# A third key tile shared between VectorE and a transfer, moved loads, and a reordered ones product at the seam of attention and MLP

## The chip, the cores and the metric

The kernel runs on one core of one Trainium2 chip. The metric is device time in microseconds (us) for one launch. Before the change the median of three timed runs is 902.75 us (901.11 to 903.17). The profiled execution took 899.86 us, and its trace spans 898.0 us from the first to the last instruction.

## The reference

Bucketed attention is followed by an MLP with a PReLU. With B = 4, H = 8, S = 768 and D = 64:

```python
mask = q_bucket[:, :, :, None] == k_bucket[:, :, None, :]   # 6 sign bits of q @ proj, k @ proj
scores = np.where(mask, scale * np.matmul(q, k.transpose(0, 1, 3, 2)), -1000000000.0)
attn = np.exp(scores - np.max(scores, axis=-1, keepdims=True))
attn = attn / (np.sum(attn, axis=-1, keepdims=True) + 1e-09)
x = np.matmul(attn, v)                                      # to (B*S, H*D) = (3072, 512)
h = x @ w_in                                                # w_in 512 x 2048
g = np.maximum(h, 0.0) + alpha * np.minimum(h, 0.0)
return g @ w_out                                            # w_out 2048 x 512
```

What matters for the change is the row sum of `attn`: for every query, the exponentials over 768 keys have to be added up, and the attention output divided by the result.

## The kernel before

**Attention, 16 pairs.** `fast_path` works through 16 pairs, each one batch entry and two heads (pairs 0 to 3 are batch entry 0). In a pair, TensorE computes scores in 12 cells (6 key tiles of 128 keys by 2 halves of 384 queries). The product of the hash bits and the product of q and k add up in one PSUM tile, and ScalarE writes the exponential (L737) into `pts[kc]`, one tile for each key tile, 128 partitions by 4 rows of 384. Then TensorE multiplies the exponentials with v (`attend`, L768) into the PSUM tile `av`.

**The row sums.** VectorE adds the six key tiles elementwise. `add_first` (L745) puts tiles 0 and 1 into `accp`. For every pair but the first, tile 2 is then added to `accp` by an accumulating transfer that GpSimd issues (L747). `add_last` (L751, L752) puts tiles 3, 4 and 5 into `accd`, and `add_total` (L757) adds `accp` to `accd`. After `attend`, `totals` (L782) sums `accd` over the 128 partitions by a product with ones into the PSUM tile `sm`. `divide` then transposes `sm` (L798), takes reciprocals, and writes the divided output `x` (L815), which is stored to `x_s` in device memory. `divide` of a pair runs on VectorE during the scores of the next pair.

**Buffers around it.** The PSUM tag `sc` has three double banks. Scores, hash bits, turned inputs and `sm` rotate through them, so a later cell of the next pair waits until L798 has read `sm`. `av` has one buffer, so the next `attend` waits for L815.

**Weights.** Between these steps VectorE splits the weights into float32 parts, two pieces of 512 columns per pair (L587 to L624). For `w_in` it also forms sums (L644), which SyncE stores to `w_in_s` (L649).

**The MLP.** Each product is a seven-product scheme over 2 x 2 blocks (`Product.step`; the numbers are those of the seven products). The first product, `ff1(0, 0)`, takes the weight tile `wi` of `load_w(0)` (L846, 896 KB) and four loaded blocks of batch entry 0 (`load_x(0, n)`, L830, 384 KB each: n = 0, 1, 2, 3 give blocks 0, 1, 2, 5). VectorE derives the other three blocks and block 5 anew (`sum_x`, L840): step 0 is block 3 = block 5 - block 0, step 1 is block 5 = block 2 - block 5. Steps 0 and 1 are in pair 13, and steps 2 and 3 in pair 14. Before the change, `load_x` is in pairs 9, 10, 11 and 12 in the order of n, and `load_w(0)`, `load_w(1)` and `load_w(2)` are in pairs 12, 13 and 14.

**What sets the order.** `do(...)` pins an instruction behind the instruction traced before it on its own engine. All VectorE, TensorE and ScalarE work here is pinned, so these engines run in program order. Transfers on SyncE are mostly not pinned and are issued in an order chosen when the kernel is built, but `load_x(0, n)` and the first three `load_w` are pinned behind the transfer written just before them. In pair 13 that is the load of v for pair 15, `load(15, "v")` (L487), which needs the v buffer of pair 13.

**The seam.** In the last pair (15) TensorE does `attend`, then products 1 and 5 of the first MLP block (`now.step(1)`, `now.step(5)`), then `totals(15)`, and after that products 6, 3, 7 and 2. Product 2 (`f_0b`) writes to the PSUM bank that `av` held, so it waits for L815 of pair 15.

Of the kernel before, what the change touches and what calls it, by code (L numbers as in the profile page):

```python
# [12 lines left out]
ALU = mybir.AluOpType  # L13
# [393 lines left out]
def fast_path(  # L407
# [12 lines left out]
    nc = tc.nc  # L420
# [21 lines left out]
    do = tc.keep_in_program_order  # L442
    PE, DVE, ACT, POOL = nc.tensor, nc.vector, nc.scalar, nc.gpsimd
# [36 lines left out]
    accp, accd, av, vsum, sums = {}, {}, {}, {}, {}  # L480
# [102 lines left out]
    def weight_clamp(i):  # L583
        if i < NW:
            i = order[i]
            x = wx[i]
            do(DVE.tensor_scalar(x, x, HI_MIN, None, op0=ALU.max, op1=ALU.max, accum_out=wmax[:, i : i + 1]))  # L587

    def weight_parts(i):
        i = order[i]  # L590
        lo, hi = halves(i)
        x = wx[i]
        wr[i] = r = pool.tile([P, 512], F32, name=f"wr{i}", tag="wr", bufs=1)
        do(DVE.tensor_scalar(
            x.bitcast(U32), x.bitcast(U32), 3, 0xC0000000, op0=ALU.logical_shift_left, op1=ALU.bitwise_xor,
        ))
        do(DVE.tensor_scalar(r.bitcast(U32), x.bitcast(U32), 0x7F800000, None, op0=ALU.bitwise_and))
        do(DVE.scalar_tensor_tensor(r, lo, 2.0 ** -52, r, op0=ALU.mult, op1=ALU.mult))

    def weight_sum(i):  # L600


        i = order[i]
        lo, hi = halves(i)
        x, r = wx[i], wr[i]
        if i < HW:
            n, m = divmod(i, 4)
            if m == 0:
                wst[n] = pool.tile([P, NM, 4, P], F32, name=f"wsi{n}", tag="wsi")
            slot = (0, 5, 1, 2)[m]  # L610
            dst = wst[n][:, slot].rearrange("p i f -> p (i f)")
        else:
            n, m = divmod(i - HW, 2)
            if m == 0:
                wst[HW + n] = pool.tile([P, 4, DM // 2], F32, name=f"wso{n}", tag="wso")
            w = wst[HW + n]
            dst = w[:, 0:4:3] if m == 0 else w[:, 1:3]
        turned = i < HW and m == 3
        do(DVE.scalar_tensor_tensor(
            r, x, -1.0 if turned else 1.0, r, op0=ALU.mult, op1=ALU.subtract if turned else ALU.add,  # L620
        ))
        if i >= HW:
            hi, r = (t.rearrange("p (a f) -> p a f", a=2) for t in (hi, r))
        do(DVE.scalar_tensor_tensor(  # L624
            dst.bitcast(U32), hi, 0x80000000, r.bitcast(U32), op0=ALU.bitwise_and, op1=ALU.bitwise_xor,
        ))
# [99 lines left out]
    def scores(pi, cells):  # L726
        for kc, g in cells:
            sc = two_banks(f"sc{pi}_{kc}_{g}")
            ks = slice(kc * P, (kc + 1) * P)
            qs = slice(g * CW, (g + 1) * CW)  # L730
            for what, first in ((bits, True), (tr, False)):
                for s in range(2):
                    r = slice(D * s, D * s + D)
                    do(PE.matmul(  # L734
                        sc[:, s, :CW], what["k", pi][r, ks], what["q", pi][r, qs], start=first, stop=not first,
                    ))
            do(ACT.activation(pts[kc][:, g, :, :CW], sc[:, :, :CW], AF.Exp, scale=SCALE / DOWN))  # L737


    def p(kc):  # L740
        return pts[kc].rearrange("p g s w -> p (g s) w")[:, :, :CW]

    def add_first(pi):
        accp[pi] = pool.tile([P, 2 * NCH, CW], F32, name=f"accp{pi}", tag="accp", bufs=1)
        do(DVE.tensor_tensor(accp[pi], p(0), p(1), op=ALU.add))  # L745
        if pi:
            nc.gpsimd.dma_start(accp[pi], p(2), accum_op=ALU.add)  # L747

    def add_last(pi):
        accd[pi] = pool.tile([P, 2 * NCH, CW], F32, name=f"accd{pi}", tag="accd", bufs=1)  # L750
        do(DVE.tensor_tensor(accd[pi], p(3), p(4), op=ALU.add))  # L751
        do(DVE.tensor_tensor(accd[pi], accd[pi], p(5), op=ALU.add))  # L752
        if not pi:
            do(DVE.tensor_tensor(accp[pi], accp[pi], p(2), op=ALU.add))

    def add_total(pi):
        do(DVE.tensor_tensor(accd[pi], accd[pi], accp[pi], op=ALU.add))  # L757
# [29 lines left out]
    def divide(pi, between=lambda: None):  # L787

        b, hp = pairs[pi]
        n = HW2 // 32
        a = pool.tile([P, NCH, HW2], F32, name=f"st{pi}", tag="st", bufs=1)
        r = pool.tile([P, NCH, n], F32, name=f"rc{pi}", tag="rc")
        rr = pool.tile([P, NCH, 2, n], F32, name=f"rr{pi}", tag="rr")
        d = pool.tile([P, NCH, CW], F32, name=f"dn{pi}", tag="dn", bufs=1)
        for g in range(NCH):
            do(DVE.transpose(a[:, g], sums[pi][:, g, :HW2]))  # L798
        do(DVE.tensor_scalar(r, a.rearrange("p g (n w) -> p g n w", w=32)[:, :, :, 0], S * EPS, None, op0=ALU.add))
        for h in range(2):  # L800
            do(DVE.reciprocal(rr[:, :, h], r))
        for q0 in (0, D):
            q1 = q0 + 32
            do(POOL.tensor_copy(rr[q0 : q0 + 32, :, 1], rr[q1 : q1 + 32, :, 1]))
            do(POOL.tensor_copy(rr[q1 : q1 + 32, :, 0], rr[q0 : q0 + 32, :, 0]))
        vsum[pi] = pool.tile([P, 1], F32, name=f"vs{pi}", tag="vs")
        do(DVE.tensor_scalar(vsum[pi], av[pi][:, 0, CW : CW + 1], EPS, None, op0=ALU.mult))
        between()
        do(DVE.transpose(
            d.rearrange("p g w -> p (g w)"),  # L810
            rr.rearrange("p g h n -> p (g h n)").unsqueeze(2).to_broadcast([P, 2 * NCH * n, 32]),
        ))

        x = mid.tile([P, NCH, CW], F32, name=f"x{pi}", tag="x", bufs=1)
        do(DVE.scalar_tensor_tensor(x, av[pi][:, :, :CW], vsum[pi], d, op0=ALU.add, op1=ALU.mult))  # L815
        nc.sync.dma_start(x_s[b, hp], x.rearrange("p g w -> p (g w)"))
# [4 lines left out]
    def pinned(when, ins):  # L821

        if when:
            do(ins)

    def load_x(b, *ns):
        for n in ns or range(4):
            m, kh, ch = ((0, 0, 0), (1, 1, 0), (2, 1, 1), (5, 0, 1))[n]
            t = mid.tile([P, 2, CW], F32, name=f"x{b}_{m}", tag=f"x{m}", bufs=1)
            pinned(b == 0, nc.sync.dma_start(  # L830
                t, x_s[b, 2 * kh : 2 * kh + 2].rearrange("k p s -> p k s")[:, :, ch * CW : (ch + 1) * CW],
            ))
            x_m[b, m] = t
# [8 lines left out]
    def load_w(n):  # L842

        if n < B * NI:
            w_m[n] = mid.tile([P, NM, 2, P], F32, name=f"wi{n}", tag="wi", bufs=3)
            pinned(n < 3, nc.sync.dma_start(w_m[n], w_in_s[n % NI]))  # L846
# [285 lines left out]
    for pi in range(NPAIR):  # L1132
        i = 2 * pi

        def weight_begin():
            weight_clamp(i)
            weight_parts(i)
            add_first(pi)

        scores(pi, [c for c in CELLS if pi or c not in ahead])  # L1140
        if pi:
            divide(pi - 1, weight_begin)
        else:
            add_first(pi)
        weight_sum(i)
        weight_group(i)
        load_weight(i + 3)
        if pi == 0:
            weight_abs(1, DVE)
        weight_clamp(i + 1)  # L1150
        add_last(pi)
        weight_parts(i + 1)
        weight_sum(i + 1)
        weight_group(i + 1)
        load_weight(i + 4)
        add_total(pi)
        weight_sums(2)
        if pi + 1 < NPAIR:
            hash_bits(pi + 1)
        if pi + 2 < NPAIR:  # L1160
            turn(pi + 2, "q")
            turn(pi + 2, "k")
        attend(pi)
        if pi + 1 == NPAIR:
            now = ff1(0, 0)
            now.step(1)
            now.step(5)
        totals(pi)
        if pi + 1 == NPAIR:
            divide(pi)  # L1170
        else:
            weight_abs(i + 2)
        if pi + 2 < NPAIR:
            load(pi + 2, "v")
        if 12 <= pi < 15:
            load_w(pi - 12)
        if 9 <= pi < 13:
            load_x(0, pi - 9)
        if pi in (13, 14):
            for n in range(2):  # L1180
                sum_x(0, 2 * pi - 26 + n, DVE)
        if pi == 1:
            setup_alpha()
        for name in "qk":
            magnitude(pi, name)
            if pi + 3 < NPAIR:
                load(pi + 3, name)
        if pi + 1 < NPAIR:
            weight_abs(i + 3)
# [10 lines left out]
    for j, (b, what, n) in enumerate(blocks):  # L1200
# [50 lines left out]
        if j + 1 < len(blocks):  # L1251
            b1, what1, n1 = blocks[j + 1]
            now = ff1(b1, n1) if what1 == "1" else ff2(b1, n1)
# [33 lines left out]
```

## Time and profile before

| what | value | where it is read |
|---|---|---|
| span of the profiled execution, mean granted TensorE clock | 898.0 us, 0.998 | cores |
| one pair, from L745 to L745 (pairs 12 to 13) | 283.57 - 262.96 = 20.61 us | timeline of VectorE |
| end of L757 in pair 13, start of `totals(13)` | 297.38 us, 299.05 us | timelines of VectorE and TensorE |
| end of `attend(14)`, start of `totals(14)` | 318.38 us, 321.97 us | timeline of TensorE |
| start of product 2 of the first MLP block | 348.57 us | timeline of TensorE |
| accumulating transfer of tile 2: issue to landing | 7.5 / 9.1 / 13.6 us (least, median, most of 15) | transfers of L747 |
| its landing in pairs 13, 14 and 15 | 9.0, 13.6 and 7.5 us | the same, by window |

The page has one line per engine with its busy time. The view of waits has one line per pair of a waiting instruction and the one that released it: total time, how often, and the longest. A timeline line has the start, the time from the start of the first to the end of the last instruction, the engine, the line of the kernel, what it writes and reads, and in brackets how long the engine was idle before it and who ended that.

### The profile page before, as it was taken

How to read it: one execution, taken by the hardware profiler on the slowest of the kernel's cores; microseconds unless marked ns; L12 is line 12 of the kernel's file. 1: busy time of each engine (PE TensorE's matmuls, PEld its weight loads, DVE VectorE, ACT ScalarE, POOL GpSimd, SP SyncE). 2: the span in 40 equal slices, each digit the busy share in tenths (PEclk: the TensorE clock that was granted, in tenths of full speed). 3: DMA queues.
4: the chain of work that ended last, by engine and by line, in shares of the span. 5: the costliest groups of instructions: out<-in, count | busy, mean ns of one | idle time of the engine just before them, and what ended most of it. 6: DMA issues, size and time to landing. Idle time of an engine off the chain costs nothing.

```text
span 898.0 us, 15360 instructions
## 1 busy us (share of the span) xinstructions
PE 883.2 (98%) x5886; PEld 594.6 (66%) x5886; DVE 744.0 (83%) x1251; ACT 407.4 (45%) x726; POOL 47.5 (5%) x109
## 2 busy tenths in 40 slices
PE   9999999999999989999999999999999999999996
PEld 5444455555545445557997557997557997556996
DVE  5888878878888986899898668988668988768985
ACT  7888888888888852222112222112222112222111
POOL 0100001101100001120000000000000000000000
PEclk9999999999999999999999999999999999999999
DMA  8576797797898954487333435343525242520241
GB/s 226 133 191 169 186 255 187 175 251 194 206 261 232 293 125 168 167 285 289 132 121 108 162 107 169 108 145 89 179 89 190 96 156 80 166 106 0 95 157 58
DMA packets 128817, 146.06 MB, mean 163 GB/s; under 512 B 77776, under 2 KB 112864, under 8 KB 125152
## 3 DMA queue, kind: packets, MB, share of 16 engines
q1 hardware_dynamic: 116368, 123.90, 43.7%
q0 software_dynamic: 10224, 20.19, 10.5%
q8 instruction: 48, 0.79, 0.4%
q10 hardware_dynamic: 2144, 0.92, 0.4%
q14 instruction: 33, 0.27, 0.1%
HBM read 104.87 MB, written 28.31 MB: 148 GB/s over the span
## 4 chain that ended last, share of the span: by engine, by line
PE 53%; DMA 3%; DVE 3%; issue 1%; SPq 0%; POOL 0%; ACT 0%; DVEq 0%; POOLq 0%; ACTq 0%
PE z_3a L868 2%; PE z_6a L868 2%; PE z_5a L868 2%; PE f_2a L868 2%; PE f_1a L868 2%; PE z_2a L868 2%; PE f_3a L868 2%; PE z_7a L868 2%; PE f_0a L868 2%; PE z_1a L868 2%; PE z_4a L868 2%; PE f_7a L868 2%; PE f_6a L868 2%; PE f_5a L868 2%; PE f_4a L868 2%; DMA w_out_s<-wo 2%
## 5 line engine op out<-in xcount | busy, mean ns | idle before, releaser
L737 ACT ACTIVATE pt<-sc 128x768 f32<-128x768 f32 x192 | 154.9, 812 | 37.6 <-PE sc L734 37.4
L734 PE MATMUL sc<-qT,kT 64*128 64x384 f32 x768 | 155.2, 482 | 0.0
L768 PE MATMUL av<-pt,vn 128*32 128x385 f32 (+1 forms) x1536 | 127.4, 486 | 0.0
L768 PEld LDWEIGHTS av<-pt,vn 128*32 128x32 f32 x1536 | 48.7, 109 | 71.1 <-issue 70.1
L734 PEld LDWEIGHTS sc<-qT,kT 64*128 64x128 f32 x768 | 68.1, 187 | 39.2 <-issue 39.0
L921 DVE TENSOR_TENSOR g<-g,g 128x384 f32<-128x384 f32 x128 | 68.4, 555 | 2.2
L734 PE MATMUL sc<-qb,kb 64*128 64x384 bf16 x384 | 63.3, 323 | 0.3 <-DVE kb L719 0.2
L985 DVE TENSOR_TENSOR gs<-g,gs 128x768 f32<-128x768 f32 x56 | 53.3, 952 | 1.0
L985 DVE TENSOR_TENSOR gs<-g 128x768 f32<-128x768 f32 x56 | 53.3, 951 | 0.0
L977 DVE TENSOR_TENSOR ws<-wl 128x512 f32<-128x512 f32 x56 | 38.5, 688 | 17.4 <-DMA wl<-w_out_s 15.9
L917 DVE SCALAR_TENSOR_TENSOR g<-h,alpha 128x384 f32<-128x384 f32 x32 | 19.7, 617 | 26.1 <-ACT h L910 26.1
L734 PEld LDWEIGHTS <-kb 64*128 64x128 bf16 x384 | 19.0, 94 | 28.1 <-issue 4.3
L745 DVE TENSOR_TENSOR accp<-pt,pt 128x1536 f32<-128x1536 f32 x16 | 28.1, 1758 | 10.1 <-ACT pt L737 10.1
L712 ACT ACTIVATE qb<-hs,hb 32x384 bf16<-32x384 f32 x60 | 34.4, 573 | 1.1
L757 DVE TENSOR_TENSOR accd<-accd,accp 128x1536 f32<-128x1536 f32 x16 | 28.1, 1755 | 8.1 <-DMA accp<-pt 8.1
L752 DVE TENSOR_TENSOR accd<-accd,pt 128x1536 f32<-128x1536 f32 x16 | 28.1, 1758 | 1.7
L751 DVE TENSOR_TENSOR accd<-pt,pt 128x1536 f32<-128x1536 f32 x16 | 28.0, 1753 | 0.0
L723 ACT ACTIVATE kb<-hs,hb 64x384 bf16<-64x384 f32 (+1 forms) x45 | 26.0, 577 | 0.6
L798 DVE STREAM_TRANSPOSE st<-sm 128x192 f32<-128x192 f32 x32 | 10.3, 361 | 18.4 <-PE sm L782 18.4
L868 PE MATMUL f_0a<-x,wi 128*128 128x384 f32 x64 | 23.5, 489 | 0.0
L868 PE MATMUL f_5a<-x,wi 128*128 128x384 f32 x64 | 23.3, 486 | 0.0
L868 PE MATMUL f_2a<-x,wi 128*128 128x384 f32 x64 | 23.3, 486 | 0.0
(351 smaller groups left out, 1775.8 us busy)
## 6 DMA issues: line engine op xcount, KB each, us to landing
wi<-w_in_s SPq DMA_DIRECT2D x32, 896.0 KB, 4.7
wl<-w_out_s SPq DMA_DIRECT2D x16, 1024.0 KB, 4.8
wl<-w_out_r SPq DMA_DIRECT2D x12, 1024.0 KB, 4.8
accp<-pt POOLq DMA_DIRECT2D x15, 768.0 KB, 9.1
raw<-in_moe_w_out_dram SPq DMA_DIRECT2D x16, 512.0 KB, 6.9
raw<-in_moe_w_in_dram SPq DMA_DIRECT2D x16, 512.0 KB, 4.7
w_in_s<-wsi SPq DMA_DIRECT2D x16, 448.0 KB, 5.8
vn<-in_v_dram SPq DMA_DIRECT2D x16, 384.0 KB, 4.5
```

Of the source, the lines that this page charges most:

```text
L712: do(ACT.activation(bits["q", pi][D * s : D * s + 32, cols], ps["q"][c : c + 32, 0 if engine is DVE else half, :CW], AF.Sign, bias=hb[c : ...
L734: do(PE.matmul(sc[:, s, :CW], what["k", pi][r, ks], what["q", pi][r, qs], start=first, stop=not first,))
L737: do(ACT.activation(pts[kc][:, g, :, :CW], sc[:, :, :CW], AF.Exp, scale=SCALE / DOWN))
L745: do(DVE.tensor_tensor(accp[pi], p(0), p(1), op=ALU.add))
L751: do(DVE.tensor_tensor(accd[pi], p(3), p(4), op=ALU.add))
L752: do(DVE.tensor_tensor(accd[pi], accd[pi], p(5), op=ALU.add))
L757: do(DVE.tensor_tensor(accd[pi], accd[pi], accp[pi], op=ALU.add))
L768: do(PE.matmul(av[pi][D * s + t : D * s + t + 32, g, :w], nat["v", pi][:, s, kc * D + t : kc * D + t + 32], pts[kc][:, g, s, :w], start=(k ...
L868: do(PE.matmul(self.ps[bank], self.left(left, k), self.right(right, k), start=start and k == 0, stop=k == self.nk - 1, skip_group_check=no ...
L921: do(DVE.tensor_tensor(new_g(b, to)[:, i], g_m[b, x][:, i], g_m[b, y][:, i], op=ALU.subtract))
L977: do(DVE.tensor_tensor(t, w2[b, n, x], w2[b, n, y], op=op))
L985: do(DVE.tensor_tensor(t, g2[b, n, x], g2[b, n, y], op=ALU.subtract))
```

## The change

It has three parts. In pairs 1 to 15 the transfer adds only rows 2 and 3 of the third key tile, and VectorE adds rows 0 and 1 in a new step `add_third`, ahead of `add_last`. In pair 0 VectorE adds all four rows as before, only earlier. Second, the loads of the first MLP product go to other pairs: `load_w` to pairs 9, 11 and 15, `load_x` to pairs 10 (n = 0), 12 (n = 1 and 3) and 13 (n = 2). Third, in the last pair the ones product comes between products 1 and 5 of the first MLP block instead of after both. It is meant to let the sums of a pair depend on a smaller transfer, to keep large loads out of the pairs in which other transfers are many, and to give the last `divide` more time before product 2.

```diff
         if pi:
-            nc.gpsimd.dma_start(accp[pi], p(2), accum_op=ALU.add)
+            nc.gpsimd.dma_start(accp[pi][:, 2:], p(2)[:, 2:], accum_op=ALU.add)
 ...
-        if not pi:
-            do(DVE.tensor_tensor(accp[pi], accp[pi], p(2), op=ALU.add))
+
+    def add_third(pi):
+        n = 2 if pi else 4
+        do(DVE.tensor_tensor(accp[pi][:, :n], accp[pi][:, :n], p(2)[:, :n], op=ALU.add))
 ...
         weight_clamp(i + 1)
+        add_third(pi)
         add_last(pi)
 ...
             now = ff1(0, 0)
             now.step(1)
-            now.step(5)
         totals(pi)
         if pi + 1 == NPAIR:
+            now.step(5)
             divide(pi)
 ...
-        if 12 <= pi < 15:
-            load_w(pi - 12)
-        if 9 <= pi < 13:
-            load_x(0, pi - 9)
+        if pi in (9, 11, 15):
+            load_w((9, 11, 15).index(pi))
+        if pi in (10, 12, 13):
+            load_x(0, *{10: (0,), 12: (1, 3), 13: (2,)}[pi])
         if pi in (13, 14):
             for n in range(2):
                 sum_x(0, 2 * pi - 26 + n, DVE)
```

## The prediction

> **What bounds the kernel now.** I read the page first, then the waits of TensorE, then the timelines of pairs 13 to 15. The page and the waits of TensorE:
>
> ```profile
> PE 883.2 (98%) x5886; PEld 594.6 (66%) x5886; DVE 744.0 (83%) x1251; ACT 407.4 (45%) x726; POOL 47.5 (5%) x109
> ...
> PE sm L782 <- DVE accd L757: 3.6, 1, 3.6
> ...
> PE f_0b L868 <- DVE x L815: 0.4, 1, 0.4
> ```
>
> TensorE is busy in 98% of the span, so only its idle time can be won. The change can touch two of its waits: 3.6 us once, where the ones product waits for the sums, and 0.4 us once, at product 2. The pairs follow each other at 20.61 us, which is TensorE's own work. VectorE at 83% has gaps in every pair.
>
> The long wait is in pair 14. The timeline of VectorE around it:
>
> ```profile
> 297.30 1.41 DVE L644 TENSOR_TENSOR wsi<-wsi 128x512 f32<-128x512 f32 x2
> 298.62 1.94 DVE L840 TENSOR_TENSOR x<-x,x 128x768 f32<-128x768 f32 x2
> 300.49 0.64 DVE L798 STREAM_TRANSPOSE st<-sm 128x192 f32<-128x192 f32 x2
> ...
> 304.18 1.76 DVE L745 TENSOR_TENSOR accp<-pt,pt 128x1536 f32<-128x1536 f32 x1 [0.23 <-ACT pt L737]
> ...
> 320.06 1.76 DVE L757 TENSOR_TENSOR accd<-accd,accp 128x1536 f32<-128x1536 f32 x1 [3.73 <-DMA accp<-pt]
> ```
>
> L757 was ready at 320.06 - 3.73 = 316.33 and would have ended at 318.08, just before `attend(14)` ended at 318.38. It waited for the transfer of tile 2, which took 13.6 us here against a median of 9.1. SyncE shows what was in its way:
>
> ```profile
> 298.73 3.02 SPq L649 DMA_DIRECT2D w_in_s<-wsi  x3
> 301.85 0.82 SPq L487 DMA_DIRECT2D vn<-in_v_dram  x1
> 302.71 0.49 SPq L846 DMA_DIRECT2D wi<-w_in_s  x1
> 303.25 0.53 SPq L649 DMA_DIRECT2D w_in_s<-wsi  x1
> 303.82 0.76 SPq L846 DMA_DIRECT2D wi<-w_in_s  x1
> ```
>
> Four stores of 448 KB, a load of v and two weight loads of 896 KB go out in 5 us. The last line counts twice over: `load_w(2)` is written in pair 14 but issued here. Last, the weight loads of TensorE:
>
> ```profile
> 301.18 0.10 PEld L734 LDWEIGHTS <-kb 64*128 64x128 bf16 x2 [0.19 <-DVE st L798]
> ```
>
> The third cell of pair 14 waits for L798 of pair 13, because `sm` holds one of three banks. Anything that delays L798 there stops TensorE two cells into the pair.
>
> [...] L747, issued by GpSimd, took 13.6 us in the crowd of pair 14 and 7.5 in pair 15. [...] Here the gap of 3.59 us was followed by cells at the usual 0.81 us[...].
>
> **Part 1, half of the third tile.** VectorE gains 15 adds of 128x768, 15 x 0.95 = 14.3 us in all. In an ordinary pair this is hidden: in pair 13 L757 ends at 297.38 and TensorE takes the sums at 299.05, 1.67 us later, and 0.72 is left after 0.95. The next thing on VectorE, L798, waits for `sm` anyway (18.4 us over 13 pairs). Tile 2 is long written when `add_third` runs. The halved transfer has 384 KB. I have no row for it, and bound its landing by the v loads of that size (about 4 us) and by today's median of 9.1 us. Even the latter ends before L757. It removes the six waits of L757 (8.1 us), of which only that of pair 14 reached TensorE. I assume that `add_third` does not wait for the transfer, since they touch different rows. That halves of one tile can be waited for separately, the trace suggests at the start, where the first halves of q are turned at 4.15 us and the second at 7.06.
>
> **Part 2, the moved loads.** Pair 14 loses two weight loads (1.8 MB) from its front; the loads now in pairs 9 to 12 have 20 us or more until use and cost nothing. One does not: block 2 is now loaded in pair 13, and `sum_x` step 1 of the same pair reads it. That is a new wait on VectorE. Behind it are L798, then L815, which frees `av`, and all sums of pair 14. TensorE's third cell waits for L798. The steps:
>
> - The load is pinned behind that of v for pair 15, whose buffer is free when `attend(13)` ends, at about 299.0. In pairs 9 and 10 the block load followed v by 0.76 and 0.64, so it goes out at 299.7 if no store is ahead.
> - Landing took 4.3, 5.1 and 4.7 us in pairs 9 to 11 (8.3 beside a weight load in pair 12; 3.2 is the least of 16). With 4.6 it lands at 304.3.
> - Without that wait, step 1 would start at 298.71 + 0.95 (`add_third` of pair 13) + 0.94 = 300.6. It waits 3.7 us. After its 0.95, L798 starts at 305.25 instead of 300.49.
> - From L798 to the ready L757 was 316.33 - 300.49 = 15.84. The idle 0.23 ahead of L745 goes, the new add brings 0.95: 16.56. With L757's 1.75 the sums are ready at 323.56. In the kernel before it was 320.06 + 1.76 = 321.82. That is +1.74.
> - TensorE by itself would be there sooner: the third cell to the end of `attend(14)` took 318.38 - 301.44 = 16.9, less than 18.3.
>
> **Part 3, the ones product.** It starts one product earlier (1.39 us), so L815 comes that much sooner and the 0.42 us before product 2 can go. Two things take back part. VectorE has no gap in pair 15 (321.82 to 340.92 = 19.10), and with 0.95 more it needs 20.05, while TensorE reaches the ones product after 18.48 + 1.39 = 19.87: a tie. And ScalarE copies product 5 some 0.78 us later, with 1.8 us of squares (L687) behind it and then the copy of product 6, for which product 7 waits: about 0.2. I take -0.2 in all; the bounds are 0 and -0.42.
>
> **Sum.** Change = landing of block 2 - 302.76 us: (landing + 0.95 + 18.31) - 321.82 - 0.2. At 304.3 it is +1.5, from 902.75 to **904.3 us**.
>
> **The rivals.**
>
> - *A, as above*: v and block 2 go out ahead of the stores. For it: before, VectorE's sums let the stores start at 298.73, just ahead of v; 0.95 us more on VectorE puts the stores behind. 904.3 us. Chance 0.42.
> - *B, stores first*: the order of SyncE is fixed when the kernel is built, and before three stores lead, each about 1.0 us. They would now start at 299.66. With one ahead block 2 lands at 306.1 (+3.3); with three it goes out at 303.6 and lands after 4.6 to 6.9 (what the weight load in that place took), at 308.2 to 310.5: +5.4 to +7.7. I take +5.0, 907.8. [...] Chance 0.30.
> - *C, the wait is hidden*: block 2 is there by 300.6. Then L798 starts at 301.54 and the sums are ready at 319.85, -1.97 and -0.2: 900.6 us, faster. Against it: a landing within 1 us of issue, where 3.2 is the least seen. For it in effect: the timed median lies 2.9 us above the profiled 899.86. If those are longer waits for tile 2 that the smaller transfer ends, the same sum is won in another way, down to 897.7. Chance 0.25.
> - *D, the half add waits for the transfer*, if the tile counts as a whole. Issued 2.3 us after L745 starts and landing after 5 to 9 us, it would hold `add_third` (5.5 us after L745) by 2 to 6 us, of which 0.72 is covered: over 15 pairs +17 us at least, 920. Only the start speaks against it. Chance 0.03.
>
> **Chances and range.** Faster by over 0.2% means under 900.95: most of C and little of A, 0.25. Within 0.2% (to 904.55): the lower half of A, where block 2 lands soon or some of the 2.9 us goes, 0.27. Slower: the rest of A, B and D, 0.48. The range reaches from within C to the top of B's middle cases, 899.8 to 909.0, and leaves out D, the earliest of C and three stores with a late landing.
>
> **What would show it.** Step 1 of `sum_x` in pair 13 should wait for a transfer into `x`, by 3 to 10 us, and L798 after it should be the releaser of a TensorE gap two cells into pair 14. L757 should have no wait for the transfer of tile 2, and the ordinary pairs should keep 20.61 us. Product 2 should have no wait for L815. I am wrong if block 2 is issued before `attend(13)` ends, if L757 waits for rows 2 and 3, or if ordinary pairs grow.

## The result, and the profile after

The changed kernel takes **905.39 us** (median of 6 runs, 905.05 to 908.69). The kernel before, run beside it, takes 902.12 us (6 runs, 901.10 to 904.01). The medians differ by 3.3 us. The ratio, which is taken over all the runs and not from the two medians, is 1.0041, with a 95% interval from 1.0023 to 1.0060: slower. The profiled execution has a span of 903.5 us, against 898.0 in the profile of before.

In the changed kernel the numbers of the lines concerned are higher by two: L759 is the sum L757 of before, L800 the transpose L798, L842 the step of `sum_x`, L784 the ones product. `add_third` is L756.

The page's first part:

```profile
PE 884.9 (98%) x5886; PEld 594.9 (66%) x5886; DVE 756.4 (84%) x1266; ACT 407.5 (45%) x726; POOL 46.3 (5%) x109
```

VectorE has the 15 instructions more, and 12.4 us more of busy time. TensorE's work is the same. What differs is what it waits for. The waits of TensorE, with the total, the number and the longest in us:

```profile
PE sc L734 <- DVE st L800: 5.6, 1, 5.6
...
PE sm L784 <- DVE accd L759: 0.8, 1, 0.8
```

The 3.6 us ahead of the ones product have become 0.8, and the 0.4 us at product 2 are gone. A new wait of 5.6 us stands in an earlier place, at a score product behind L800. VectorE's waits say where L800 got its delay:

```profile
DVE st L800 <- PE sm L784: 11.5, 13, 1.7
...
DVE x L842 <- DMA x<-x_s: 8.2, 1, 8.2
```

L759 isn't in the list of VectorE's long waits any more, and there is one new wait, of 8.2 us, for a transfer into `x`. VectorE's timeline at the end of pair 13 and in pair 14:

```profile
298.00 1.41 DVE L644 TENSOR_TENSOR wsi<-wsi 128x512 f32<-128x512 f32 x2
299.33 0.95 DVE L842 TENSOR_TENSOR x<-x,x 128x768 f32<-128x768 f32 x1
308.52 0.96 DVE L842 TENSOR_TENSOR x<-x,x 128x768 f32<-128x768 f32 x1 [8.24 <-DMA x<-x_s]
309.40 0.64 DVE L800 STREAM_TRANSPOSE st<-sm 128x192 f32<-128x192 f32 x2
...
318.31 0.96 DVE L756 TENSOR_TENSOR accp<-accp,pt 128x768 f32<-128x768 f32 x1
...
325.71 1.76 DVE L759 TENSOR_TENSOR accd<-accd,accp 128x1536 f32<-128x1536 f32 x1
```

Step 0 of `sum_x` runs at once. Step 1 needs block 2 and holds VectorE for 8.24 us. After that every instruction follows without a gap worth naming, `add_third` and L759 included: they don't wait for the transfer of tile 2. That transfer, of 384 KB now, landed 4.3 us after issue in this pair, where the whole tile had taken 13.6. Why block 2 came so late is in the timeline of SyncE, which issues it:

```profile
299.44 3.00 SPq L649 DMA_DIRECT2D w_in_s<-wsi  x3
302.54 1.10 SPq L487 DMA_DIRECT2D vn<-in_v_dram  x1
303.68 0.50 SPq L832 DMA_DIRECT2D x<-x_s  x1
304.22 0.53 SPq L649 DMA_DIRECT2D w_in_s<-wsi  x1
```

Three stores and the load of v are issued first. The block load goes out at 303.68 and lands 4.8 us later. TensorE in the same stretch:

```profile
310.09 0.51 PE L734 MATMUL sc<-qb,kb 64*128 64x384 bf16 x2 [5.56 <-DVE st L800]
310.36 1.51 PE L734 MATMUL sc<-qT,kT 64*128 64x384 f32 x4
...
314.84 0.82 PE L734 MATMUL sc<-qT,kT 64*128 64x384 f32 x4
...
327.62 0.86 PE L784 MATMUL sm<-accd,ones 128*32 128x192 f32 x16 [0.83 <-DVE accd L759]
```

The group of four f32 products takes 1.51 us right after the stop and 0.82 us 4.5 us later: the granted clock was 0.50 from 310 to 314 us. The ones product then starts at 327.62 and still waits 0.83 us for VectorE. Against the kernel before:

| event | before, us | after, us | difference, us |
|---|---|---|---|
| start of the transpose of `sm` in pair 13 | 300.49 | 309.40 | +8.91 |
| start of `totals(14)` | 321.97 | 327.62 | +5.65 |
| product 2 of the first block | 348.57 | 353.92 | +5.35 |
| end of the span | 898.0 | 903.5 | +5.5 |

So all of the profiled difference arises between the end of pair 13 and `totals(14)`. Ordinary pairs keep their length: L745 of pairs 12 and 13 starts at 262.80 and 283.40, 20.60 us apart.

### The profile page after: what moved, and what is told of

Read it like the earlier page. It is cut to its first block, busy times and chain, and to the rows that moved or that the text cites. A ratio compares the mean times of both kernels' runs of the same rounds, so it can differ in the third digit from the quotient of the medians.

```text
span 903.5 us, 15371 instructions
## 1 busy us (share of the span) xinstructions
PE 884.9 (98%) x5886; PEld 594.9 (66%) x5886; DVE 756.4 (84%) x1266; ACT 407.5 (45%) x726; POOL 46.3 (5%) x109
## 4 chain that ended last, share of the span: by engine, by line
PE 88%; DVE 5%; DMA 4%; issue 2%; SPq 1%; POOL 0%; ACT 0%; DVEq 0%; ACTq 0%; POOLq 0%
PE sc L734 17%; PE av L770 13%; PE f_0a L870 2%; PE z_3a L870 2%; PE z_6a L870 2%; PE z_5a L870 2%; PE f_2a L870 2%; PE f_1a L870 2%; PE z_2a L870 2%; PE f_3a L870 2%; PE z_7a L870 2%; PE z_1a L870 2%; PE z_4a L870 2%; PE f_7a L870 2%; PE f_6a L870 2%; PE f_5a L870 2%
## 5 line engine op out<-in xcount | busy, mean ns | idle before, releaser
L745 DVE TENSOR_TENSOR accp<-pt,pt 128x1536 f32<-128x1536 f32 x16 | 28.1, 1758 | 9.9 <-ACT pt L737 9.8
L759 DVE TENSOR_TENSOR accd<-accd,accp 128x1536 f32<-128x1536 f32 x16 | 28.0, 1750 | 0.0
L870 PE MATMUL f_6a<-x,wi 128*128 128x384 f32 x64 | 23.3, 486 | 0.0
L870 PE MATMUL f_7a<-x,wi 128*128 128x384 f32 x64 | 23.3, 486 | 0.0
```

The costliest lines, as they stand in the source:

```text
L870: do(PE.matmul(self.ps[bank], self.left(left, k), self.right(right, k), start=start and k == 0, stop=k == self.nk - 1, skip_group_check=no ...
```

## The experiments

Unless it says "on before", an edit is made on the changed kernel. Ratios are to the kernel before, again over all the runs. It was run on the same chip in the same series, where its medians were 901.5, 901.6 and 901.73 us (30, 25 and 25 runs).

### Block 2 loaded one pair earlier

```diff
-        if pi in (10, 12, 13):
-            load_x(0, *{10: (0,), 12: (1, 3), 13: (2,)}[pi])
+        if pi in (10, 12):
+            load_x(0, *{10: (0,), 12: (1, 3, 2)}[pi])
```

> The changed kernel with block 2 loaded in pair 12 instead of pair 13, nothing else. Theory W (the wait of VectorE for block 2 is the whole loss): no wait ahead of the second step of sum_x; the transpose of sm starts at about 301.3 us instead of 309.4, the sums of pair 14 end 18.1 later at 319.4 instead of 327.5, TensorE has no stop inside the scores of pair 14, and the span falls by 8.1 from 903.5 to about 895.4 us, 897.5 per launch: faster than before. Rival V (the added VectorE work is what costs): the sums stay late in all pairs, the launch stays above 902. Rival S (the crowd of stores delays tile 2 of pair 14 anyway): the wait for the accumulating transfer comes back, about 900.

Measured: 896.46 us, ratio 0.9939 (0.9926 to 0.9951), span 894.9. VectorE's timeline has no wait at step 1, and the chain behind it comes early:

```profile
300.72 0.64 DVE L800 STREAM_TRANSPOSE st<-sm 128x192 f32<-128x192 f32 x2
...
317.08 1.78 DVE L759 TENSOR_TENSOR accd<-accd,accp 128x1536 f32<-128x1536 f32 x1
```

L800 starts 8.68 us sooner than in the changed kernel, and the span is 8.6 us shorter. The 5.6 us stop of TensorE is 0.4:

```profile
301.42 0.34 PE L734 MATMUL sc<-qb,kb 64*128 64x384 bf16 x2 [0.44 <-DVE st L800]
```

One load, moved by one pair, turns a loss of 0.4% into a gain of 0.6%: the wait for block 2 is the whole loss.

### The order of SyncE: stores behind the loads

The last four stores are pinned with `do` to their place in the written order (`id` leaves a transfer as it is) and go out at 321.77 us, so they are no longer ahead of v and block 2.

```diff
-                nc.sync.dma_start(w_in_s[4 * c + ii][:, :, kk], w[:, :, ii])
+                (do if n == 3 else id)(nc.sync.dma_start(w_in_s[4 * c + ii][:, :, kk], w[:, :, ii]))
```

> The changed kernel with the last four stores to w_in_s pinned in program order on their queue, so that they go out in pair 14 after the loads of v and block 2. It sets the order that case A of the prediction assumed. Theory W with the stores as the reason for the late landing: block 2 goes out at about 299.7, lands at about 304.3, VectorE waits about 4.0 us instead of 8.2, and the span is about 4.2 shorter, 899.3 us, 901.2 per launch; the stop of TensorE in pair 14 is under 2 us and its clock stays full. If the order of the queue does not matter, block 2 still lands at about 308.5 and the time stays at 905.4.

Measured: 900.72 us, ratio 0.9989 (0.9982 to 0.9996), span 898.8. SyncE:

```profile
298.78 0.38 SPq L487 DMA_DIRECT2D vn<-in_v_dram  x1
299.21 0.46 SPq L832 DMA_DIRECT2D x<-x_s  x1
```

VectorE:

```profile
304.06 0.96 DVE L842 TENSOR_TENSOR x<-x,x 128x768 f32<-128x768 f32 x1 [4.14 <-DMA x<-x_s]
```

TensorE:

```profile
305.63 0.50 PE L734 MATMUL sc<-qb,kb 64*128 64x384 bf16 x2 [2.58 <-DVE st L800]
305.90 1.51 PE L734 MATMUL sc<-qT,kT 64*128 64x384 f32 x4
```

Block 2 goes out 4.47 us earlier than in the changed kernel, the landing again takes 4.8 us, and the wait falls from 8.24 to 4.14 us. L759 of pair 14 ends at 322.99, 1.17 us later than in before. This is the order of the prediction's case A, with waits near its size; the span is 0.8 us above that of the first profile of before, where the prediction's sum gives +1.5. The stop was longer than expected, and the granted clock was 0.50 from 306 to 308 us, after 2.58 us without work.

### The first part alone, on before

The edit is the one on L747 and `add_third` in the diff above.

> The kernel before with part 1 alone (half of the third tile added by VectorE, half by the transfer). Theory W: the adds are hidden in ordinary pairs (20.61 us each as before), the sums of pair 14 end at about 319.9 instead of 321.8, so about 2 us faster than before, 900.1; up to 4 us faster if the 2.3 us by which the timed runs of before lie above its profiled one are longer waits for tile 2. Rival V: slower than before, by up to 0.95 us in each of 14 pairs. Rival D (the half add waits for the transfer): slower by 17 us or more.

Measured: 897.27 us, ratio 0.9950 (0.9936 to 0.9964), span 895.4. VectorE:

```profile
317.70 1.76 DVE L759 TENSOR_TENSOR accd<-accd,accp 128x1536 f32<-128x1536 f32 x1
```

TensorE:

```profile
319.60 0.86 PE L784 MATMUL sm<-accd,ones 128*32 128x192 f32 x16 [0.81 <-DVE accd L759]
```

There is no wait for the transfer any more, although in this crowded pair 14 (with its two weight loads) the half tile took 10.8 us to land. An ordinary pair keeps its length (20.60 us from pair 12 to 13). TensorE waits for the added work only in pair 14: 0.4 us for L800 in the scores, and 0.81 us for the sums.

### The second part alone, on before

The edit is the last hunk of the diff above, the conditions of `load_w` and `load_x`.

> The kernel before with part 2 alone (the moved loads). Theory W: block 2 goes out at about 302.7 behind three stores and v, lands at about 307.5, VectorE waits about 7.5 us for it, and the sums of pair 14 end at about 325.8 instead of 321.8: 4 us slower than before, 906; only 2 us slower, 904, if the timed runs of before have longer waits than its profile. Rival V: without the added VectorE work the loads cost nothing and the freed weight loads bring tile 2 in sooner, about 899.

Measured: 904.22 us, ratio 1.0027 (1.0017 to 1.0038), span 902.4. VectorE:

```profile
308.63 0.96 DVE L840 TENSOR_TENSOR x<-x,x 128x768 f32<-128x768 f32 x1 [8.44 <-DMA x<-x_s]
```

The loss sits in this part, and the wait is there without the other two.

### The third part alone, on before; and the first and third together

The third part is the move of `now.step(5)`.

> The kernel before with part 3 alone (the ones product of the last pair between products 1 and 5). By the prediction's step: the 0.42 us before product 2 goes, and up to 0.2 us comes back where product 7 waits for the copy of product 6: 0.2 to 0.4 us faster, hardly to be told from no change. Rival: the later copy of product 5 holds up the products, 0.2 us slower or more.

Measured: 900.75 us, ratio 0.9994 (0.9986 to 1.0001): not told from no change. In the profile product 2 no longer waits.

> The changed kernel without part 2: half of the third tile by VectorE and the reordered ones product, but all loads in their old pairs. Theory W: as with the half alone (897.3), less 0.2 to 0.4 us: 897.0, and within 1 us of the changed kernel with block 2 in pair 12 (896.5), so that moving the loads brings next to nothing once the transfer of tile 2 is halved. Rival S: the two weight loads at the head of pair 14 still cost, and this is 1.5 us or more above 896.5.

Measured: 896.99 us, ratio 0.9949 (0.9936 to 0.9963). It leaves out the second part, and is within 0.53 us of the version that has all three with block 2 in pair 12. Once the transfer is halved, moving the loads brings nothing that can be measured.

### The loads moved, block 2 in pair 12, nothing else, on before

```diff
-        if 12 <= pi < 15:
-            load_w(pi - 12)
-        if 9 <= pi < 13:
-            load_x(0, pi - 9)
+        if pi in (9, 11, 15):
+            load_w((9, 11, 15).index(pi))
+        if pi in (10, 12):
+            load_x(0, *{10: (0,), 12: (1, 3, 2)}[pi])
```

> The kernel before with the moved loads, but block 2 in pair 12; no half tile, no reordered ones product. Theory W: without two weight loads at its head, pair 14 has tile 2 about 9.2 us after the issue at 306.4, at about 315.7, before L757 is ready at 316.3; the wait of 3.6 us goes and with it the halved clock: about 896.8, as good as the half tile alone (897.3), so that either remedy alone is enough. Rival: the four stores are the crowd, tile 2 still lands late by 2 us or more, and it stays at 899 or above.

Measured: 896.14 us, ratio 0.9943 (0.9930 to 0.9957), span 894.4. VectorE:

```profile
316.72 1.75 DVE L757 TENSOR_TENSOR accd<-accd,accp 128x1536 f32<-128x1536 f32 x1
```

TensorE, without a wait:

```profile
318.68 0.84 PE L782 MATMUL sm<-accd,ones 128*32 128x192 f32 x16
```

The whole tile 2 landed in 8.3 us in pair 14 instead of 13.6, with the two weight loads out of its way and the four stores still there, and L757 has no wait there. Either remedy, the smaller transfer or the emptier pair, takes away all of the 3.6 us or all but 0.8 by itself. That is why their gains don't add up.

### The clock after the gap: before once more, and before with the gap filled

The kernel before was profiled a second time, unchanged.

> The kernel before, unchanged, for one more profile. The timed runs of before have a median of 901.5 us against 899.9 of the profiled one. If their surplus is the wait for the transfer of tile 2, a run at 901.5 shows L757 of pair 14 waiting about 5.4 us instead of 3.7 and the ones product about 5.2 instead of 3.6, and all else the same; if it lies elsewhere, the wait in pair 14 stays at 3.7 us and other pairs or the start are longer.

Measured: 900.14 us, span 898.4. TensorE at `totals(14)`:

```profile
321.47 1.51 PE L782 MATMUL sm<-accd,ones 128*32 128x192 f32 x16 [3.65 <-DVE accd L757]
```

In the first profile of before:

```profile
321.97 0.86 PE L782 MATMUL sm<-accd,ones 128*32 128x192 f32 x16 [3.59 <-DVE accd L757]
```

The gap is the same 3.6 us, and tile 2 landed 13.6 us after issue in both, but the ones product takes 1.51 us in the second and 0.86 in the first. A window of the trace just after it shows the busy time and count of PE, PEld, DVE, ACT and POOL, then the granted clock, the DMA share and GB/s. In this second profile:

```profile
322.00:324.00 2.00, 2.00 (x21) 1.02 (x12) 1.90 (x6) 0.00 (x0) 0.00 (x0) 0.50 0.00 0
```

and in the first profile of before:

```profile
322.00:324.00 2.00, 2.00 (x26) 1.26 (x28) 1.97 (x4) 0.15 (x1) 0.00 (x0) 1.00 0.00 0
```

From `totals(14)` to product 1 it is 341.55 - 321.47 = 20.08 us with the halved clock and 340.45 - 321.97 = 18.48 without: 1.6 us. Over the whole execution the second profile took only 0.28 us longer (900.14 against 899.86), so other parts of a run vary by about as much. The next kernel fills the gap with 16 products of a tile of zeros (the one that the kernel sets at its start, kept in `zeros`), ahead of the ones product of pair 14, on before.

```diff
-    nil = []
+    nil, zeros = [], []
...
-        do(DVE.memset(zero, 0.0))
+        do(DVE.memset(zero, 0.0)); zeros.append(zero)
...
+        for _ in range(16 if pi == 14 else 0): do(PE.matmul(sums[pi][:, 0], zeros[0][:, :P], zeros[0], start=True, stop=True))
```

> The kernel before with 16 products of a zero tile (128x512 bf16[...]) written into the tile sm ahead of the ones product of pair 14, in the gap in which TensorE waits for the sums. Theory K (the timed runs of before lie above its first profile because the gap of 3.6 us halves the clock of TensorE for some 3.4 us in most runs, costing about 1.6 us): the clock stays full, the median falls from 901.6 to about 900.0, and the runs spread less. If the surplus is a longer wait for tile 2 in other runs, the median stays at 901.6.

Measured: 900.24 us over 21 runs, ratio 0.9982 (0.9975 to 0.9988). TensorE:

```profile
318.79 3.63 PE L778 MATMUL sm<-zero 128*128 128x512 bf16 x16
322.77 0.86 PE L783 MATMUL sm<-accd,ones 128*32 128x192 f32 x16 [0.36 <-DVE accd L757]
```

and the window after it:

```profile
322.00:324.00 2.00, 1.64 (x22) 0.79 (x22) 1.97 (x3) 0.00 (x0) 0.00 (x0) 1.00 0.00 0
```

Useless products made the kernel 1.5 us faster, with the sums no sooner: VectorE still waited 4.2 us for tile 2. All 21 runs have a mean granted clock of 0.997 or 0.998. Of the 80 runs of before in the three series, 12 have that:

| mean granted clock of a run of before | runs | median time, us |
|---|---|---|
| 0.993 and 0.994 | 13 | 902.40 |
| 0.995 | 17 | 901.79 |
| 0.996 | 38 | 901.49 |
| 0.997 and 0.998 | 12 | 900.32 |

The first profile of before, on which the prediction rests, also has 0.998, as only 4 of these 80 runs do.

### Two steps further

One block is loaded in each of the pairs 9 to 12, in the order n = 0, 3, 2, 1, and one step of `sum_x` is done in each of the pairs 11 to 14, instead of two in each of 13 and 14:

```diff
-        if pi in (10, 12, 13):
-            load_x(0, *{10: (0,), 12: (1, 3), 13: (2,)}[pi])
-        if pi in (13, 14):
-            for n in range(2):
-                sum_x(0, 2 * pi - 26 + n, DVE)
+        if 9 <= pi < 13:
+            load_x(0, (0, 3, 2, 1)[pi - 9])
+        if 11 <= pi < 15:
+            for n in range(1):
+                sum_x(0, pi - 11, DVE)
```

> The changed kernel with the loads of the blocks 0, 5, 2, 1 in pairs 9, 10, 11, 12 and the four steps of sum_x one by one in pairs 11, 12, 13, 14 instead of two each in 13 and 14. Every block has a pair's time to land. Theory W: with block 2 in pair 12 TensorE still waited 0.44 us for the transpose of sm and 0.65 us for the sums of pair 14, both because VectorE does two steps between two pairs; with one step both go: about 1.1 us less than 896.5, 895.4. If these waits come from the added half tile alone, it stays at 896.5.

Measured: 896.42 us, ratio 0.9943 (0.9929 to 0.9956), span 894.6. The expected gain didn't come. The wait of 0.4 us for L800 went, but TensorE still waits 0.6 us for the sums of pair 14: L745 waits 0.36 us for an exponential of ScalarE, and from there to L759's end (304.11 to 318.82) VectorE works for 14.7 us without a gap. So the sums can come earlier only if VectorE has less to do in that pair. The last kernel adds this: in pair 14 the transfer takes the whole third tile and VectorE none.

```diff
-            nc.gpsimd.dma_start(accp[pi][:, 2:], p(2)[:, 2:], accum_op=ALU.add)
+            n = 0 if pi == 14 else 2
+            nc.gpsimd.dma_start(accp[pi][:, n:], p(2)[:, n:], accum_op=ALU.add)
...
-        do(DVE.tensor_tensor(accp[pi][:, :n], accp[pi][:, :n], p(2)[:, :n], op=ALU.add))
+        if pi != 14: do(DVE.tensor_tensor(accp[pi][:, :n], accp[pi][:, :n], p(2)[:, :n], op=ALU.add))
```

> As sums_spread (896.4), but in pair 14 alone the transfer takes the whole third tile and VectorE adds nothing of it. Pair 14 has no inputs to turn, so TensorE is there sooner, and the added 0.95 us of VectorE is what made TensorE wait 0.65 us there. Theory W: that wait goes, 895.8. If the whole transfer lands late again (more than 10 us after its issue), the wait comes back in another form and it is no faster than 896.4.

Measured: **895.56 us**, ratio 0.9931 (0.9917 to 0.9945), span 893.8. TensorE has no wait before the ones product of pair 14:

```profile
318.64 0.84 PE L785 MATMUL sm<-accd,ones 128*32 128x192 f32 x16
```

With pair 14 free of the weight loads, the whole tile lands in 8.7 us, in time. It has the lowest median of all versions and beats both kernels; against the five other versions between 896.1 and 897.3 us its interval doesn't decide. In its own series all five of its runs (894.85 to 895.81) lie below the five of the version with the loads moved alone (895.89 to 897.27).

## Why the prediction was right and where it was wrong

**Mechanism: right.** The new wait for block 2 at step 1 of `sum_x`, the delay of L800 behind it, the stop of TensorE in pair 14 and the late sums are all in the profile. Loading block 2 one pair sooner takes them away but for 0.4 us of the stop and 0.65 us before the ones product, and the second part alone brings them.

**The choice between A and B: wrong.** The step that failed is "so it goes out at 299.7 if no store is ahead". Case A argued that 0.95 us more on VectorE would put the stores behind. The stores did start 0.7 us later, but three of them still led, as in before, since the order of SyncE's queue is fixed when the kernel is built: case B's reason, to which the prediction gave less weight. Block 2 went out at 303.68 and landed at about 308.5, in case B's stretch, and not at 304.3. The landing after issue was well sized (4.8 for 4.6). With the stores put last, the wait and the sums take case A's size: 4.14 us for the predicted 3.7, and +1.17 us at L759's end for +1.74.

**The formula: right.** "Landing minus 302.76" gives +5.7 us at 308.5. The two profiles differ by 5.5. Its largest term, from the start of L800 to the ready sums, was put at 18.31 us and measured 18.07 (309.40 to 327.47).

**The base: wrong, and it hid the first error.** The prediction added its change to 902.75, a timed median 2.9 us above the profile of 899.86 from which the change was worked out, and offered longer waits for tile 2 as the reason in case C. In the second profile of before, tile 2 of pair 14 took no longer to land (13.6 us in both). By an estimate from their mean granted clock (0.996 or less in 68 of 80 runs, 0.996 in the second profile, 0.998 in the first), most runs of before have a halved clock after the gap of 3.6 us. That cost 1.6 us where two profiles could be compared, and filling the gap brings 1.5 us while the wait for tile 2 remains. What the changed kernel does to the timed median is therefore less than the two profiles show: +5.5 us, less the 2.26 us by which the median of before (902.12) exceeds that one good profile, is +3.2, and +3.3 was measured. The changed kernel's own profile took 905.33 us, close to its median of 905.39. So the 904.3 came near the result by luck, by two errors of opposite sign: +4.2 us of landing left out, and a base 2.9 us above the profile to which the change belongs (904.3 + 4.2 - 2.9 = 905.6). With the profile as base, case A would have come out at about 901.4, and the kernel with case A's order did take 900.72. By an estimate from the filled gap (901.73 to 900.24 us), the clock explains about 1.5 of the 1.6 to 2.3 us by which the medians of before exceed its first profile. What makes up the rest isn't settled.

**The place of the stop: wrong, at no cost.** TensorE was to stop at the third cell of pair 14. It stopped at the sixth, after two short waits of 0.17 and 0.15 us for ScalarE: the third and fifth cell waited for banks that ScalarE frees, and only the sixth, for 5.56 us, for the one that `sm` held. VectorE's chain sets the sums either way. The halved clock after this stop probably cost nothing, since TensorE still waited 0.83 us for the sums; this is argued from that wait and wasn't tried by itself. A small cost isn't excluded: with the stores late, the six runs at a mean granted clock of 0.997 or 0.998 have a median of 900.2 us, and the 16 others 900.9.

**Part 1: right.** The adds (0.95 us each: a median of 953 ns at `add_third` with the first part alone, against 954 in the mean at L840 in before) are hidden in ordinary pairs, and the halved transfer is always early: median 4.7 us to landing, within the bounds of 4 and 9.1, and at most 8.4 (10.8 with the first part alone, over the bound but still in time). Case C's end of the sums, 319.85, is 319.46 with the first part alone, and its lower bound of 897.7 us is near that kernel's 897.27. The surplus that it took for longer waits is for the most part the halved clock after the gap, which goes with the gap. Case D didn't occur: L756 never waits for the transfer.

**Part 3: right in size.** The wait of product 2 is gone, and the products 3 to 7 give back 0.18 us (352.53 - 351.06 = 1.47, against 1.29 before) where 0.2 was predicted. Its effect on the time can't be told from no change.

## What to carry to other kernels

When a load is moved, look at what else is in its queue at the new place, in the order in which it was built, and leave a whole stage between it and the instruction that an in-order engine can't pass: 8 us at one small add delayed the sums of the next stage by almost 6. Two remedies for one wait didn't add up here (897.27 and 896.14 us each alone, 896.46 with both and the third part), so test each alone before keeping both. Read a gap's price from several runs and their clocks; a single profile can show an execution in which the gap was cheap, as the first one of before did (18.48 us from `totals(14)` to product 1, against 20.08 in the second).

## What the runs showed of the hardware

- A gap of 3.6 us was followed by a whole clock in one profile of before (granted clock 1.00 from 322 to 324 us) and by a halved one in another (0.50 in the same window). Summed over windows of 1 and 2 us, the clock stayed halved for 3.4 us in the second profile of before and with the stores late, and for 6.8 us in the changed kernel, whose stop was 5.56 us. With the stores late the gap was 2.58 us, with one wait of 0.17 us two cells before it, and the clock was halved some 2.1 us after the gap began.
- With sixteen useless products of 128x512 in that gap, 3.63 us in all, the granted clock was 1.00 from 320 to 328 us in the profile, and the mean granted clock 0.997 or more in all 21 runs.
- The accumulating transfer of 768 KB took 7.5 to 13.6 us in the first profile of before, the longest in pair 14, where two weight loads go out ahead of it; with those loads in other pairs it took 8.3 us there (the loads moved, block 2 in pair 12, nothing else) and 8.7 us (the last kernel). 384 KB had a median of 4.7 us in the changed kernel and 5.2 with the first part alone, where the slowest took 10.8, beside two weight loads.
